# A sliding-window attention and MLP kernel on one core: normalisation split in two, a plain weight cast, shifted V by DMA, a padded first key block

## The chip, the cores and the metric

The kernel runs on one core of a Trainium2 chip. The metric is the device time of the program in microseconds (us); lower is better. A *span* is the time from the first to the last instruction of one profiled execution; it is about 1.7 us shorter than the time of the same run. Most runs of a kernel agree within about 1%; runs over 1.5% above the fastest of their kernel count as slow and are left out of the ratios (the medians are of all runs).

The engines are named as the profile names them: PE is TensorE (matrix products), PEld its weight loads, DVE is VectorE, ACT is ScalarE, POOL is GpSimd, SP is SyncE, which here issues the loads and stores. In the traces of this case each engine takes up its own instructions in program order and waits where an operand is not ready: POOL, for example, once stands idle for 17.15 us in front of one instruction with more work behind it (shown below). The *granted clock* is the share of full speed that the profile records for PE. An *eviction* copies a result of PE out of the memory that PE writes to.

## The reference

Eight batches of 576 rows, 8 heads of 64. Attention looks back over a window of 64 keys, then the rows go through a normalised two-layer MLP with a residual:

```python
scores = q @ k.T / sqrt(64)                    # (8, 8, 576, 576)
mask   = (0 <= i - j) & (i - j < 64)
attn   = softmax(where(mask, scores, -1e9))
x      = (attn @ v) as (8, 576, 512)           # heads side by side

xn  = (x - mean(x)) / sqrt(var(x) + 1e-6) * g_ln      # over the 512
out = x + relu(xn @ w_ch1) @ w_ch2                    # 512 -> 2048 -> 512
```

## The kernel before

Work is cut into 36 blocks of 128 rows. Four blocks form a *group*, and the MLP runs on nine groups of 512 rows. While PE works on the 32 *slots* of group g (16 units of the first layer, then 16 of the second, 4 matmuls each), the attention of batch g+1 is threaded between the slots. The parts that the change and the argument touch (cuts are marked):

```python
def make_vB(b, lo, hi):            # V shifted by 64 rows, for even windows
    nc.vector.tensor_copy(out=vB[b][64:128, lo:hi], in_=vA[b][0:64, lo:hi])
    ...
def w1_cast(i):                    # fp32 -> fp16, times g
    for e in range(2):
        nc.gpsimd.tensor_scalar(out=w1g[...], in0=t[:, e], scalar1=gcol[:, kc:kc+1], op0=ALU.mult)

def s_mm(b, ws):                   # scores of one or two windows, then exp
    k0 = 64 if ws[0] == 0 else 0   # window 0 has no earlier keys: half a key block
    ...
def s_mask(b, ws):                 # DVE: probabilities *= mask
    ...
def b_step(kblk):                  # one block of 128 rows
    # PE: xps = P @ [V, 1], 16 matmuls; then on DVE:
    #   rcp = 1/sum;  xn = xps*rcp;  bn_stats;  bn_aggr -> mean, var
    ...
def group_stats(g):                # DVE, once per group, after its fourth block
    # 12 ops on 128x4: rs = 1/sqrt(var + eps) by two Newton steps
    for kb in range(4):            # z = (xn - mean) * rs
        nc.vector.tensor_scalar(out=z, in0=xn, scalar1=mean, scalar2=rs, ...)
def zt_step(g, pr):                # PE: transposes of two blocks' z; DVE: eviction to zT
    ...
# second layer, per block:         DVE: out = ch + xn, then store

# groups g >= 1, b = g + 1, s0 = 10 (cut):
for i, ws in enumerate([[0], [1, 2], [3, 4], [5, 6], [7, 8]]):
    at(s0 + 2*i, s_mm, b, ws)
    at(s0 + 2*i + 1, s_mask, b, ws)
# b_step of a block 2 slots after the s_mm of its last window
# group_stats 1 slot, zt_step 3 and 4 slots after the group's last block
```

The *fill* is what comes before group 1: loads and casts of W1 and W2, batch 0's attention, then group 0, which also carries batch 1's attention in its second layer.

The softmax here doesn't subtract the row's maximum and nothing guards it: scores larger than these inputs give would overflow.

Of the kernel before, what the change touches and what calls it, by code (L numbers as in the profile page):

```python
# [20 lines left out]
def kernel(  # L21
# [44 lines left out]
    gcol = p_const.tile([128, NKC], FP32, tag="gcol", name="gcol")  # L66
# [6 lines left out]
    x_norm, zT, mvg, zsd = {}, {}, {}, {}  # L73
# [56 lines left out]
    def alloc_vB(b):  # L130
        vB[b] = p_va.tile([128, 5, H, D + 1], FP16, tag="vB", name=f"vB_{b}")

    def make_vB(b, lo, hi):
        nc.vector.tensor_copy(out=vB[b][64:128, lo:hi], in_=vA[b][0:64, lo:hi])
        l1 = max(lo, 1)
        if l1 < hi:
            nc.vector.tensor_copy(out=vB[b][0:64, l1:hi], in_=vA[b][64:128, l1 - 1:hi - 1])
# [13 lines left out]
    def w1_cast(i):  # L151
        q2, pr = divmod(i, 2)
        t = wst.pop(("w1", i))
        for e in range(2):
            kc = 2 * pr + e
            nc.gpsimd.tensor_scalar(  # L156
                out=w1g[:, kc, (HID // 4) * q2:(HID // 4) * (q2 + 1)], in0=t[:, e],
                scalar1=gcol[:, kc:kc + 1], scalar2=None, op0=ALU.mult,
            )
# [11 lines left out]
    def alloc_qkT(b):  # L171
        qkT[b] = [p_qkt.tile([128, NHP, S], FP16, tag=f"qkT{x}", name=f"qkT{x}_{b}") for x in range(2)]
# [7 lines left out]
    def t_main(b, x, half):  # L180
# [5 lines left out]
        evac(x, qkT[b][x][:, 2 * half:2 * half + 2, 0:512].rearrange("c i (p j) -> c i p j", j=4),  # L186
             tp[:, :].rearrange("c i j p -> c i p j"))

    def t_rem(b):
# [6 lines left out]
        for x in range(2):  # L196
            nc.vector.tensor_copy(out=qkT[b][x][:, :, 512:S], in_=tp[:, x])

    def s_mm(b, ws):
        nw = len(ws)  # L200
        k0 = 64 if ws[0] == 0 else 0
        sc = [ps_s.tile([128, NHP, nw, 64], FP32, tag="sc", name=f"sc_{b}_{ws[0]}_{par}") for par in range(2)]
        pt = p_pt.tile([128, 2, NHP, nw, 64], FP16, tag=f"pt{nw}", name=f"pt_{b}_{ws[0]}", bufs=6 if nw == 2 else 3)
        for hp in range(NHP):
            for iw, w in enumerate(ws):
                for par in range(2):
                    rows = slice(64 * par, 64 * par + 64)
                    nc.tensor.matmul(
                        out=sc[par][k0:, hp, iw, :],
                        lhsT=qkT[b][1][rows, hp, max(0, 64 * (w - 1)):64 * (w + 1)],  # L210
# [3 lines left out]
        for par in range(2):  # L214
            nc.scalar.activation(out=pt[k0:, par], in_=sc[par][k0:], func=AF.Exp, bias=0.0, scale=scale)
        for iw, w in enumerate(ws):
            pts[(b, w)] = (pt, iw, k0)

    def s_mask(b, ws):
        pt, _, k0 = pts[(b, ws[0])]  # L220
        m = mask[k0:, :]
        mb = bass.AP(tensor=m.tensor, offset=m.offset, ap=[m.ap[0], [0, 2 * NHP * len(ws)], m.ap[1]])
        ptv = pt[k0:].rearrange("p a h w i -> p (a h w) i")
        nc.vector.tensor_tensor(out=ptv, in0=ptv, in1=mb, op=ALU.mult)

    def v_rhs(b, w, h, k0):
        if w % 2 == 1:
            return vA[b][:, (w - 1) // 2, h, :]
        return vB[b][k0:, w // 2, h, :]

    def b_step(kblk):
# [5 lines left out]
        for h in range(H):  # L237
            par, hp = h % 2, h // 2
            for r, (b, w) in enumerate(halves):
                pt, iw, k0 = pts[(b, w)]  # L240
                nc.tensor.matmul(
                    out=xps[64 * r:64 * r + 64, h, :D + 1],
                    lhsT=pt[k0:, par, hp, iw, :], rhs=v_rhs(b, w, h, k0),
# [11 lines left out]
        nc.vector.bn_aggr(out=mvg[g][:, kb, :], in_=stats)  # L255

    def group_stats(g):
        mv = mvg[g]
        rs = p_grp.tile([128, 4], FP32, tag="rstdg", name=f"rstdg_{g}")
        tmp = p_grp.tile([128, 4, 3], FP32, tag="rstmp", name=f"rstmp_{g}")  # L260
        ve = tmp[:, :, 0]
        hv = tmp[:, :, 1]
        ab = tmp[:, :, 2]
        nc.vector.tensor_scalar(out=ve, in0=mv[:, :, 1], scalar1=EPS, scalar2=None, op0=ALU.add)
        nc.vector.tensor_scalar(out=hv, in0=mv[:, :, 1], scalar1=0.5, scalar2=0.5 * EPS,
                                op0=ALU.mult, op1=ALU.add)
# [5 lines left out]
                                in1=ab.bitcast(I32), op=ALU.subtract)  # L272
        for _ in range(2):
            nc.vector.tensor_tensor(out=ab, in0=rs, in1=rs, op=ALU.mult)
            nc.vector.tensor_tensor(out=ab, in0=ab, in1=hv, op=ALU.mult)
            nc.vector.tensor_scalar(out=ab, in0=ab, scalar1=-1.0, scalar2=1.5, op0=ALU.mult, op1=ALU.add)
            nc.vector.tensor_tensor(out=rs, in0=rs, in1=ab, op=ALU.mult)
        zs = []
        for kb in range(4):
# [63 lines left out]
    for i in range(4):  # L343
        w1_load(i)
# [157 lines left out]
```

## Time and profile before

| | before |
|---|---|
| median time | 420.46 us (4 runs, 417.25 to 421.12) |
| second layer of group 0 starts | 66.2 us |
| first layer of group 1 starts | 99.45 us |
| groups 1 to 6, each | 41.7 to 44.2 us, 258.0 us in sum |
| groups 7 and 8, without attention, and the tail | 28.6, 27.7, about 4 us |

The starts are those of the first-layer matmuls in the timeline of PE. Lines of the page of the kernel before; the second row gives PE's granted clock in tenths, in 40 equal slices of the span:

```profile
span 417.7 us, 6727 instructions
PE 349.5 (84%) x2768; PEld 175.5 (42%) x2768; DVE 203.8 (49%) x440; ACT 139.3 (33%) x243; POOL 101.6 (24%) x107
PEclk9999995898999999899898989999999999999999
```

Busy time in three stretches of the kernel before. The columns are named in the first line, each engine with its instruction count in brackets, then granted clock, share of the DMA engines and GB/s. The first two rows lie in the fill, the third is one steady group:

```profile
core 0: us, PE busy (x) PEld busy (x) DVE busy (x) ACT busy (x) POOL busy (x), PEclk, DMA share, GB/s
20.00:30.00 10.00, 3.94 (x75) 2.81 (x75) 8.52 (x19) 1.74 (x4) 10.00 (x7) 1.00 0.52 161
90.00:100.00 10.00, 4.68 (x44) 2.15 (x42) 8.88 (x27) 0.00 (x0) 0.00 (x0) 0.94 0.10 29
184.96:228.75 43.79, 40.49 (x321) 20.12 (x320) 22.96 (x49) 15.84 (x28) 8.05 (x9) 0.92 0.42 106
```

At 20 to 30 us POOL is busy all the time with W1 and DMA is half idle. At 90 to 100 us DVE is the busy one. In the steady group the clock is only 0.92.

The same group in the chain of waits (start, length, engine, what). `xps` is attention times V, `hps` the first layer, `ch` the second, `pt` the masked probabilities:

```profile
201.44 2.34 PE xps_2342 L241 x16
203.78 1.00 PE hps_15_2369 L308 x4
204.78 1.71 PE ch_0_2376 L321 x4
...
207.03 0.60 PE xps_2403 L241 x16
...
212.24 0.55 DVE z_2449 L282
...
216.53 0.61 DVE pt_7_2464 L224
...
217.18 0.45 PE xps_2542 L241 x15
217.63 4.38 PE ch_1_2526 L321 x12
```

Four second-layer matmuls take 0.86 us elsewhere in this group. The first `xps`, the one with the half key block, takes 2.34 us for 16 matmuls where others take about 0.45 to 0.6; the four `ch_0` matmuls after it take 1.71 us, half speed. Twelve later ones take 4.38 us instead of 2.6. Between them a DVE run (statistics of the group, four z, a mask) holds PE up. A wait of PE in the fill, before the second layer of group 0, for batch 1's last rows of q and k (engine, tile, line, what it waited for: sum, count, longest):

```profile
PE tpr_701 L194 <- POOL qkr_0_1_634 L104: 6.3, 1, 6.3
```

And all of its waits in the steady group above:

```profile
PE xps_2542 L241 <- DVE pt_7_2464 L224: 1.9, 1, 1.9
PE ztp_0_2516 L296 <- DVE z_2449 L282: 1.3, 1, 1.3
```

### The profile page before, as it was taken

The page shows a single profiled execution, that of the slowest core. Times are in us where ns is not written, and L with a number is a line of the kernel's source. Part 1 is how long each engine was busy: PE and PEld are TensorE (multiplying, and loading weights), DVE is VectorE, ACT ScalarE, POOL GpSimd, SP SyncE. Part 2 cuts the span into 40 slices and gives each one's busy share as a digit, 9 for nine tenths or more (in the row PEclk, how much of TensorE's full clock was granted, in tenths as well). Part 3 has the DMA queues.
Part 4 walks back from the last instruction along what each step waited for, and adds up shares of the span by engine and source line. Part 5 has one row for each costly group of instructions (what it writes and reads, how often), then busy time and mean ns, then how long its engine had stood idle before and what let it go on. Part 6 is the DMA issues. An engine that isn't in the chain of part 4 may idle for free.

```text
span 417.7 us, 6727 instructions
## 1 busy us (share of the span) xinstructions
PE 349.5 (84%) x2768; PEld 175.5 (42%) x2768; DVE 203.8 (49%) x440; ACT 139.3 (33%) x243; POOL 101.6 (24%) x107
## 2 busy tenths in 40 slices
PE   1733967976997998699969997899789968999996
PEld 1521432433453544344534543355335433444442
DVE  1488041685559347825492539443944385412001
ACT  2310550222750374016510752057205630440620
POOL 4799946400500250024002320133002000000000
PEclk9999995898999999899898989999999999999999
DMA  8959899604406450458016800872071001102002
GB/s 232 274 166 282 252 268 239 165 27 157 97 2 138 140 163 2 92 127 223 2 42 148 251 2 2 172 234 38 0 171 45 2 2 50 53 0 75 27 25 75
DMA packets 72942, 46.57 MB, mean 111 GB/s; under 512 B 47824, under 2 KB 64208, under 8 KB 72912
## 3 DMA queue, kind: packets, MB, share of 16 engines
q1 hardware_dynamic: 72384, 46.15, 41.3%
q8 instruction: 21, 0.34, 0.4%
q14 instruction: 9, 0.07, 0.1%
q10 hardware_dynamic: 528, 0.00, 0.1%
HBM read 36.70 MB, written 9.44 MB: 110 GB/s over the span
## 4 chain that ended last, share of the span: by engine, by line
PE 60%; DVE 22%; POOL 8%; SPq 4%; DMA 2%; issue 2%; POOLq 0%
POOL w1g L156 6%; SPq L114 3%; PE ch_0_712 L321 1%; DMA w1s_118<-in_moe_w_ch_dram 1%; DMA qk32r_1_273<-in_k_dram 1%; PE ch_1_2526 L321 1%; PE ch_1_2016 L321 1%; POOL w2s L169 1%; PE ch_3_4563 L321 1%; PE ch_2_4543 L321 1%; PE ch_1_4346 L321 1%; PE ch_3_3659 L321 1%; PE ch_2_3121 L321 1%; PE ch_2_2077 L321 1%; PE ch_3_1571 L321 1%
## 5 line engine op out<-in xcount | busy, mean ns | idle before, releaser
L308 PEld LDWEIGHTS <-w1g 128*128 128x128 f16 x576 | 54.0, 99 | 62.6 <-issue 9.0
L321 PEld LDWEIGHTS <-hrT_522 128*128 128x128 f16 x64 | 6.7, 113 | 9.1 <-issue 5.0
L321 PEld LDWEIGHTS <-hrT_2133 128*128 128x128 f16 x64 | 6.6, 107 | 8.5 <-issue 3.0
L321 PEld LDWEIGHTS <-hrT_1599 128*128 128x128 f16 x64 | 6.4, 105 | 8.0 <-issue 2.3
L321 PEld LDWEIGHTS <-hrT_4186 128*128 128x128 f16 x64 | 6.3, 98 | 7.5
L321 PEld LDWEIGHTS <-hrT_4406 128*128 128x128 f16 x64 | 6.2, 97 | 7.6
L327 DVE TENSOR_TENSOR osb_4520<-ch_0_4503,xn_3938 128x512 f32<-128x512 f32 x1 | 0.7, 692 | 16.7 <-PE ch_0_4503 L321 16.7
L321 PEld LDWEIGHTS <-hrT_3687 128*128 128x128 f16 x64 | 6.0, 98 | 6.7
L321 PEld LDWEIGHTS <-hrT_2643 128*128 128x128 f16 x64 | 6.0, 98 | 6.7
L321 PEld LDWEIGHTS <-hrT_3177 128*128 128x128 f16 x64 | 6.0, 98 | 6.7
L321 PEld LDWEIGHTS <-hrT_1089 128*128 128x128 f16 x64 | 5.9, 98 | 6.5
L125 POOL CAST vA_3166<-v_6_3107 128x2048 f16<-128x2048 f32 x1 | 1.9, 1892 | 27.8 <-DMA v_6_3107<-in_v_dram 27.8
L125 POOL CAST vA_2122<-v_4_2063 128x2048 f16<-128x2048 f32 x1 | 1.9, 1892 | 26.2 <-DMA v_4_2063<-in_v_dram 26.2
L125 POOL CAST vA_3676<-v_7_3617 128x2048 f16<-128x2048 f32 x1 | 1.9, 1892 | 25.7 <-DMA v_7_3617<-in_v_dram 25.7
L125 POOL CAST vA_2632<-v_5_2573 128x2048 f16<-128x2048 f32 x1 | 1.9, 1892 | 25.6 <-DMA v_5_2573<-in_v_dram 25.6
L125 POOL CAST vA_1588<-v_3_1529 128x2048 f16<-128x2048 f32 x1 | 1.9, 1893 | 24.0 <-DMA v_3_1529<-in_v_dram 24.0
L178 DVE COPY qkT_1_590<-tp_1_0_607 128x1024 f16<-128x1024 f16 x1 | 1.2, 1224 | 13.2 <-PE tp_1_0_607 L185 13.2
L312 ACT ACTIVATE hrT_2133<-hps_0_2134 128x512 f16<-128x512 f32 x1 | 0.6, 597 | 19.0 <-PE hps_0_2134 L308 19.0
L312 ACT ACTIVATE hrT_2643<-hps_0_2644 128x512 f16<-128x512 f32 x1 | 0.6, 597 | 18.8 <-PE hps_0_2644 L308 18.8
L312 ACT ACTIVATE hrT_522<-hps_0_523 128x512 f16<-128x512 f32 x1 | 0.6, 597 | 17.9 <-PE hps_0_523 L308 17.9
L185 PE MATMUL tp_0_0_143<-ident_99,qk_0_0_0_139 128*128 128x128 f16 x8 | 1.0, 310 | 6.5 <-POOL qk_0_0_0_139 L95 6.5
L296 PE MATMUL ztp_0_502<-ident_99,z_493 128*128 128x128 f16 x4 | 0.6, 308 | 6.7 <-DVE z_493 L282 6.7
(1275 smaller groups left out, 952.6 us busy)
## 6 DMA issues: line engine op xcount, KB each, us to landing
v_0_113<-in_v_dram SPq DMA_DIRECT2D x4, 256.0 KB, 7.5
v_1_262<-in_v_dram SPq DMA_DIRECT2D x4, 256.0 KB, 7.1
v_2_812<-in_v_dram SPq DMA_DIRECT2D x4, 256.0 KB, 5.2
v_3_1529<-in_v_dram SPq DMA_DIRECT2D x4, 256.0 KB, 4.6
v_4_2063<-in_v_dram SPq DMA_DIRECT2D x4, 256.0 KB, 4.3
v_5_2573<-in_v_dram SPq DMA_DIRECT2D x4, 256.0 KB, 4.5
v_6_3107<-in_v_dram SPq DMA_DIRECT2D x4, 256.0 KB, 4.5
v_7_3617<-in_v_dram SPq DMA_DIRECT2D x4, 256.0 KB, 5.6
```

What stands on the lines that cost most here:

```text
L114: nc.sync.dma_start(out=v32[b][:, c], in_=v[b, :, 128 * c:128 * c + 128, :].rearrange("h s d -> s h d"),)
L125: nc.gpsimd.tensor_copy(out=vA[b][:, c0:c1, :, 0:D], in_=v32[b][:, c0:c1])
L156: nc.gpsimd.tensor_scalar(out=w1g[:, kc, (HID // 4) * q2:(HID // 4) * (q2 + 1)], in0=t[:, e], scalar1=gcol[:, kc:kc + 1], scalar2=None, op ...
L169: nc.gpsimd.tensor_copy(out=w2s[:, 2 * i:2 * i + 2, :], in_=wst.pop(("w2", i)))
L178: nc.vector.tensor_copy(out=out, in_=in_)
L185: nc.tensor.transpose(out=tp[:, i, j, :], in_=src[:, i, j], identity=ident16)
L296: nc.tensor.transpose(out=ztp[:, kc, i, :], in_=zs[2 * pr + i][:, 128 * kc:128 * (kc + 1)], identity=ident16)
L308: nc.tensor.matmul(out=hps, lhsT=w1g[:, kc, 128 * hc:128 * (hc + 1)], rhs=zT[g][:, kc, :], start=(kc == 0), stop=(kc == NKC - 1),)
L312: nc.scalar.activation(out=hrT[:, hc, :], in_=hps, func=AF.Relu, bias=0.0, scale=1.0)
L321: nc.tensor.matmul(out=ch[kb], lhsT=hrT[:, hc, 128 * kb:128 * (kb + 1)], rhs=w2s[:, hc, :], start=(hc == 0), stop=(hc == NHC - 1),)
L327: nc.vector.tensor_tensor(out=o, in0=ch[kb], in1=x_norm[kblk][:, :, :].rearrange("p h d -> p (h d)"), op=ALU.add,)
```

## The change

Its intent: take GpSimd's slow W1 multiply out of the fill, dissolve the DVE run at the end of each group, take copies off DVE, and stop PE from alternating between half and whole key blocks. Since 1/sqrt(var + eps) is positive, it commutes with the ReLU and both matrix products, so it can be applied once at the output. The diff, cut to its core:

```diff
-        nc.vector.tensor_copy(out=vB[b][64:128, lo:hi], in_=vA[b][0:64, lo:hi])
+        nc.gpsimd.dma_start(out=vB[b][64:128, lo:hi], in_=vA[b][0:64, lo:hi])
         ...
-        for e in range(2):
-            nc.gpsimd.tensor_scalar(... scalar1=gcol[:, kc:kc + 1], op0=ALU.mult)
+        nc.gpsimd.tensor_copy(out=w1g[:, 2*pr:2*pr+2, ...], in_=t)        # W1 plain
         ...
+        nc.gpsimd.memset(vB[b][0:64, 0], 0.0)                 # in alloc_vB
+        nc.gpsimd.memset(qkT[b][1][:, :, 0:64], 0.0)          # in alloc_qkT: 64 zero keys
-        k0 = 64 if ws[0] == 0 else 0
-        lhsT=qkT[b][1][rows, hp, max(0, 64 * (w - 1)):64 * (w + 1)]
+        lhsT=qkT[b][1][rows, hp, 64 * w:64 * w + 128]
         ...
+        # in b_step, per block:  z = (xn - mean) * g
+        nc.vector.scalar_tensor_tensor(out=z, in0=xn, scalar=mean, in1=gB, ...)
         ...
     def group_stats(g):            # 3 ops on DVE, then 9 on GpSimd; no z
-            nc.vector.tensor_tensor(out=ab, in0=rs, in1=rs, op=ALU.mult)  # and so on
+            nc.gpsimd.tensor_tensor(out=ab, in0=rs, in1=rs, op=ALU.mult)  # and so on
         ...
-                nc.vector.tensor_tensor(out=o, in0=ch[kb], in1=xn, op=ALU.add)
+                nc.vector.scalar_tensor_tensor(out=o, in0=ch[kb], scalar=rstd, in1=xn,
+                                               op0=ALU.mult, op1=ALU.add)
         ...
+        at(13, group_stats, g)
-            t0, s0 = 0, 10
+            t0, s0, sp = 0, 6, 3          # groups >= 1; group 0: 10, 20, 2
-                si = s0 + 2 * ((lastw + 1) // 2) + 2
+                si = s0 + sp * ((lastw + 1) // 2) + 3
                 at(min(si, 32), b_step, kblk)
+                at(max(min(si + 4, 32), ...), zt_step, kblk)
```

More of the change, by code (lines that the diff above doesn't have):

```diff
@@ L65 @@
     magt = p_const.tile([128, 4], FP32, tag="magt", name="magt")
-    gcol = p_const.tile([128, NKC], FP32, tag="gcol", name="gcol")
+    gB = p_const.tile([128, DM], FP32, tag="gB", name="gB")
     w1g = p_const.tile([128, NKC, HID], FP16, tag="w1g", name="w1g")
@@ L72 @@
     qkT, vA, vB, pts = {}, {}, {}, {}
-    x_norm, zT, mvg, zsd = {}, {}, {}, {}
+    x_norm, zT, mvg, zsd, rstd = {}, {}, {}, {}, {}
     def load_qk(b, half):
@@ L131, in alloc_vB @@
         vB[b] = p_va.tile([128, 5, H, D + 1], FP16, tag="vB", name=f"vB_{b}")
+        nc.gpsimd.memset(vB[b][0:64, 0], 0.0)
     def make_vB(b, lo, hi):
-        nc.vector.tensor_copy(out=vB[b][64:128, lo:hi], in_=vA[b][0:64, lo:hi])
-        l1 = max(lo, 1)
-        if l1 < hi:
-            nc.vector.tensor_copy(out=vB[b][0:64, l1:hi], in_=vA[b][64:128, l1 - 1:hi - 1])
+        nc.gpsimd.dma_start(out=vB[b][64:128, lo:hi], in_=vA[b][0:64, lo:hi])
+        l0, l1 = max(lo - 1, 0), min(hi - 1, 4)
+        nc.gpsimd.dma_start(out=vB[b][0:64, l0 + 1:l1 + 1], in_=vA[b][64:128, l0:l1])
     wst = {}
@@ L153, in w1_cast @@
         t = wst.pop(("w1", i))
-        for e in range(2):
-            kc = 2 * pr + e
-            nc.gpsimd.tensor_scalar(
-                out=w1g[:, kc, (HID // 4) * q2:(HID // 4) * (q2 + 1)], in0=t[:, e],
-                scalar1=gcol[:, kc:kc + 1], scalar2=None, op0=ALU.mult,
-            )
+        nc.gpsimd.tensor_copy(
+            out=w1g[:, 2 * pr:2 * pr + 2, (HID // 4) * q2:(HID // 4) * (q2 + 1)], in_=t,
+        )
     def w2_load(i):
@@ L171, in alloc_qkT @@
     def alloc_qkT(b):
-        qkT[b] = [p_qkt.tile([128, NHP, S], FP16, tag=f"qkT{x}", name=f"qkT{x}_{b}") for x in range(2)]
+        qkT[b] = [p_qkt.tile([128, NHP, S + 64 * x], FP16, tag=f"qkT{x}", name=f"qkT{x}_{b}") for x in range(2)]
+        nc.gpsimd.memset(qkT[b][1][:, :, 0:64], 0.0)
     def evac(x, out, in_):
@@ L185, in t_main @@
                 nc.tensor.transpose(out=tp[:, i, j, :], in_=src[:, i, j], identity=ident16)
-        evac(x, qkT[b][x][:, 2 * half:2 * half + 2, 0:512].rearrange("c i (p j) -> c i p j", j=4),
+        evac(x, qkT[b][x][:, 2 * half:2 * half + 2, 64 * x:64 * x + 512].rearrange("c i (p j) -> c i p j", j=4),
              tp[:, :].rearrange("c i j p -> c i p j"))
@@ L196, in t_rem @@
         for x in range(2):
-            nc.vector.tensor_copy(out=qkT[b][x][:, :, 512:S], in_=tp[:, x])
+            nc.vector.tensor_copy(out=qkT[b][x][:, :, 64 * x + 512:64 * x + S], in_=tp[:, x])
     def s_mm(b, ws):
         nw = len(ws)
-        k0 = 64 if ws[0] == 0 else 0
         sc = [ps_s.tile([128, NHP, nw, 64], FP32, tag="sc", name=f"sc_{b}_{ws[0]}_{par}") for par in range(2)]
@@ L208, in s_mm @@
                     nc.tensor.matmul(
-                        out=sc[par][k0:, hp, iw, :],
-                        lhsT=qkT[b][1][rows, hp, max(0, 64 * (w - 1)):64 * (w + 1)],
+                        out=sc[par][:, hp, iw, :],
+                        lhsT=qkT[b][1][rows, hp, 64 * w:64 * w + 128],
                         rhs=qkT[b][0][rows, hp, 64 * w:64 * w + 64],
@@ L214, in s_mm, with v_rhs @@
         for par in range(2):
-            nc.scalar.activation(out=pt[k0:, par], in_=sc[par][k0:], func=AF.Exp, bias=0.0, scale=scale)
+            nc.scalar.activation(out=pt[:, par], in_=sc[par], func=AF.Exp, bias=0.0, scale=scale)
         for iw, w in enumerate(ws):
-            pts[(b, w)] = (pt, iw, k0)
+            pts[(b, w)] = (pt, iw)
     def s_mask(b, ws):
-        pt, _, k0 = pts[(b, ws[0])]
-        m = mask[k0:, :]
+        pt, _ = pts[(b, ws[0])]
+        m = mask[:, :]
         mb = bass.AP(tensor=m.tensor, offset=m.offset, ap=[m.ap[0], [0, 2 * NHP * len(ws)], m.ap[1]])
-        ptv = pt[k0:].rearrange("p a h w i -> p (a h w) i")
+        ptv = pt[:, :].rearrange("p a h w i -> p (a h w) i")
         nc.vector.tensor_tensor(out=ptv, in0=ptv, in1=mb, op=ALU.mult)
-    def v_rhs(b, w, h, k0):
+    def v_rhs(b, w, h):
         if w % 2 == 1:
             return vA[b][:, (w - 1) // 2, h, :]
-        return vB[b][k0:, w // 2, h, :]
+        return vB[b][:, w // 2, h, :]
     def b_step(kblk):
@@ L239, in b_step @@
             for r, (b, w) in enumerate(halves):
-                pt, iw, k0 = pts[(b, w)]
+                pt, iw = pts[(b, w)]
                 nc.tensor.matmul(
                     out=xps[64 * r:64 * r + 64, h, :D + 1],
-                    lhsT=pt[k0:, par, hp, iw, :], rhs=v_rhs(b, w, h, k0),
+                    lhsT=pt[:, par, hp, iw, :], rhs=v_rhs(b, w, h),
                     start=True, stop=True,
@@ L255, in b_step, with zt_step @@
         nc.vector.bn_aggr(out=mvg[g][:, kb, :], in_=stats)
+        z = p_blk.tile([128, DM], FP16, tag="z", name=f"z_{kblk}")
+        zsd[kblk] = z
+        nc.vector.scalar_tensor_tensor(
+            out=z, in0=xn[:, :, :].rearrange("p h d -> p (h d)"), scalar=mvg[g][:, kb, 0:1], in1=gB,
+            op0=ALU.subtract, op1=ALU.mult,
+        )
+    def zt_step(kblk, eng=None):
+        g, kb = divmod(kblk, 4)
+        z = zsd.pop(kblk)
+        if g not in zT:
+            zT[g] = p_grp.tile([128, NKC, 512], FP16, tag="zT", name=f"zT_{g}")
+        ztp = ps_t.tile([128, NKC, 128], FP16, tag="tp", name=f"ztp_{kblk}")
+        for kc in range(NKC):
+            nc.tensor.transpose(out=ztp[:, kc, :], in_=z[:, 128 * kc:128 * (kc + 1)], identity=ident16)
+        dst = zT[g][:, :, 128 * kb:128 * kb + 128]
+        if eng == "act":
+            nc.scalar.copy(out=dst, in_=ztp)
+        else:
+            nc.vector.tensor_copy(out=dst, in_=ztp)
     def group_stats(g):
+        rstd[g] = p_grp.tile([128, 4], FP32, tag="rstdg", name=f"rstdg_{g}")
+        rs = rstd[g]
         mv = mvg[g]
-        rs = p_grp.tile([128, 4], FP32, tag="rstdg", name=f"rstdg_{g}")
-        tmp = p_grp.tile([128, 4, 3], FP32, tag="rstmp", name=f"rstmp_{g}")
-        ve = tmp[:, :, 0]
-        hv = tmp[:, :, 1]
-        ab = tmp[:, :, 2]
+        tmp = p_grp.tile([128, 3, 4], FP32, tag="rstmp", name=f"rstmp_{g}")
+        ve, hv, ab = tmp[:, 0], tmp[:, 1], tmp[:, 2]
         nc.vector.tensor_scalar(out=ve, in0=mv[:, :, 1], scalar1=EPS, scalar2=None, op0=ALU.add)
-        nc.vector.tensor_scalar(out=hv, in0=mv[:, :, 1], scalar1=0.5, scalar2=0.5 * EPS,
-                                op0=ALU.mult, op1=ALU.add)
         nc.vector.tensor_scalar(
@@ L272, in group_stats @@
                                 in1=ab.bitcast(I32), op=ALU.subtract)
+        nc.gpsimd.tensor_scalar(out=hv, in0=mv[:, :, 1], scalar1=0.5, scalar2=0.5 * EPS,
+                                op0=ALU.mult, op1=ALU.add)
         for _ in range(2):
-            nc.vector.tensor_tensor(out=ab, in0=rs, in1=rs, op=ALU.mult)
-            nc.vector.tensor_tensor(out=ab, in0=ab, in1=hv, op=ALU.mult)
-            nc.vector.tensor_scalar(out=ab, in0=ab, scalar1=-1.0, scalar2=1.5, op0=ALU.mult, op1=ALU.add)
-            nc.vector.tensor_tensor(out=rs, in0=rs, in1=ab, op=ALU.mult)
-        zs = []
-        for kb in range(4):
-            kblk = 4 * g + kb
-            z = p_blk.tile([128, DM], FP16, tag="z", name=f"z_{kblk}")
-            nc.vector.tensor_scalar(
-                out=z, in0=x_norm[kblk][:, :, :].rearrange("p h d -> p (h d)"),
-                scalar1=mv[:, kb, 0:1], scalar2=rs[:, kb:kb + 1],
-                op0=ALU.subtract, op1=ALU.mult,
-            )
-            zs.append(z)
-        zsd[g] = zs
-        zT[g] = p_grp.tile([128, NKC, 512], FP16, tag="zT", name=f"zT_{g}")
-    def zt_step(g, pr):
-        zs = zsd[g]
-        ztp = ps_t.tile([128, NKC, 2, 128], FP16, tag="tp", name=f"ztp_{g}_{pr}")
-        for i in range(2):
-            for kc in range(NKC):
-                nc.tensor.transpose(out=ztp[:, kc, i, :], in_=zs[2 * pr + i][:, 128 * kc:128 * (kc + 1)],
-                                    identity=ident16)
-        nc.vector.tensor_copy(out=zT[g][:, :, 256 * pr:256 * pr + 256],
-                              in_=ztp[:, :, :, :].rearrange("p k i t -> p k (i t)"))
+            nc.gpsimd.tensor_tensor(out=ab, in0=rs, in1=rs, op=ALU.mult)
+            nc.gpsimd.tensor_tensor(out=ab, in0=ab, in1=hv, op=ALU.mult)
+            nc.gpsimd.tensor_scalar(out=ab, in0=ab, scalar1=-1.0, scalar2=1.5, op0=ALU.mult, op1=ALU.add)
+            nc.gpsimd.tensor_tensor(out=rs, in0=rs, in1=ab, op=ALU.mult)
     def mlp_units(g):
@@ L326, in l2 @@
                 o = p_blk.tile([128, DM], FP32, tag="osb", name=f"osb_{kblk}")
-                nc.vector.tensor_tensor(
-                    out=o, in0=ch[kb], in1=x_norm[kblk][:, :, :].rearrange("p h d -> p (h d)"), op=ALU.add,
+                nc.vector.scalar_tensor_tensor(
+                    out=o, in0=ch[kb], scalar=rstd[g][:, kb:kb + 1],
+                    in1=x_norm[kblk][:, :, :].rearrange("p h d -> p (h d)"), op0=ALU.mult, op1=ALU.add,
                 )
@@ L342 @@
     load_v(0, 0, 4)
+    nc.sync.dma_start(out=gB, in_=bass.AP(tensor=moe_g_ln.tensor, offset=moe_g_ln.offset, ap=[[0, 128], [1, DM]]))
     for i in range(4):
         w1_load(i)
-    nc.scalar.dma_start(out=gcol, in_=moe_g_ln.rearrange("(kc p) -> p kc", p=128))
     make_identity(nc, ident16)
+    nc.vector.memset(mask, 1.0)
     nc.vector.memset(magt, RSQRT_MAGIC)
-    nc.vector.memset(mask, 1.0)
     alloc_v(0)
@@ L364 @@
             t_main(0, x, half)
+    alloc_vB(0)
     for c in range(4):
         cast_v(0, c, c + 1)
+        if c % 2 == 1:
+            make_vB(0, c - 1, c + 1)
     for i in range(4):
@@ L390 @@
     cast_v(1, 0, 4)
-    alloc_vB(0)
     sets0 = [[0], [1, 2], [3, 4], [5, 6], [7]]
     s_mm(0, sets0[0])
-    for i in range(1, 5):
+    s_mm(0, sets0[1])
+    s_mask(0, sets0[0])
+    for i in range(2, 5):
         s_mm(0, sets0[i])
         s_mask(0, sets0[i - 1])
-        make_vB(0, i - 1, i)
-        if i >= 2:
-            b_step(i - 2)
+        b_step(i - 2)
+        if i >= 3:
+            zt_step(i - 3, "act")
     s_mask(0, sets0[4])
     b_step(3)
-    group_stats(0)
-    zt_step(0, 0)
-    zt_step(0, 1)
+    zt_step(2, "act")
+    zt_step(3, "act")
     for g in range(NGRP):
@@ L421 @@
             at(15, s_mask, 0, [8])
-            t0, s0 = 10, 20
+            t0, s0, sp = 10, 20, 2
         else:
-            t0, s0 = 0, 10
+            t0, s0, sp = 0, 6, 3
         if b < B:
@@ L431 @@
             at(t0 + 5, t_rem, b)
-            at(s0 + 1, alloc_vB, b)
-            at(s0 + 1, make_vB, b, 0, 5)
+            at(s0 - 1, alloc_vB, b)
+            at(s0 - 1, make_vB, b, 0, 5)
             sets = [[0], [1, 2], [3, 4], [5, 6], [7, 8]]
             for i, ws in enumerate(sets):
-                at(s0 + 2 * i, s_mm, b, ws)
-                at(s0 + 2 * i + 1, s_mask, b, ws)
+                at(s0 + sp * i, s_mm, b, ws)
+                at(s0 + sp * i + 1, s_mask, b, ws)
             first, last = (NW * b) // 2, (NW * (b + 1)) // 2
-            for i, kblk in enumerate(range(first, last)):
+            for kblk in range(first, last):
                 lastw = (2 * kblk + 1) - NW * b
-                si = s0 + 2 * ((lastw + 1) // 2) + 2
+                si = s0 + sp * ((lastw + 1) // 2) + 3
                 at(min(si, 32), b_step, kblk)
-                if kblk % 4 == 3:
-                    gg = kblk // 4
-                    if gg == b:
-                        at(min(si + 1, 32), group_stats, gg)
-                        at(min(si + 3, 32), zt_step, gg, 0)
-                        at(min(si + 4, 32), zt_step, gg, 1)
-        elif b == B:
-            at(4, group_stats, b)
-            at(8, zt_step, b, 0)
-            at(9, zt_step, b, 1)
+                at(max(min(si + 4, 32), 17 if kblk // 4 > b else 0), zt_step, kblk)
         if b + 1 < B:
```

## The prediction

> **What bounds it now.** TensorE. The chain of waits gives PE 60%, DVE 22%. By the stretches of busy time: 0 to 99 us is fill (PE 1 to 9 us busy of every 10), 99 to 358 us six nearly equal groups of 42 to 44 us, then two groups without attention at 28 us each.
>
> *Steady group, 185.1 to 228.9 us (43.8 us), from the chain.* At full clock: 128 MLP matmuls at 0.216 us = 27.6; q/k transposes 4x0.45 + 0.34; scores about 2.0; attention-times-V 4.5 blocks x 0.45; z transposes about 1.0: sum about 35. The other 8 us: PE waits for z (1.3) and for a mask multiply (1.9), both behind a DVE run of about 9 us (stats, 13 tiny ops at 0.2, four z, two evictions, output add) that all lands at once; the block with a half key window takes 2.34 us instead of 0.45, its matmuls 0.146 us apart, alternating 64- and 128-row weights; and after such gaps the clock drops: the next 4 matmuls took 1.71 us, 12 later ones 4.38 (0.36 each against 0.216). The Trainium skill names both: "TensorEngine Tiling (Array Packing)", Key Properties (changing the tiling mode drains the array) and "TensorE: Matmul & The Clock Gate", Part 1 (half rate after idle). The trace agrees.
>
> *Fill.* GpSimd's W1 multiplies (16, about 1.6 us each, 25 us) pace W1 and the weight loads behind it until 42 us; DMA is only about half busy at 20 to 30 us. PE then waits 6.3 us (until 65.3) for the last q/k remainder load of batch 1, and the second layer starts cold at 66.3. Group 1 starts at 99.45, after a DVE-bound stretch (8.9 of 10 us).
>
> **What the change does.**
> 1. W1 cast: 8 copies of 128x1024. The like W2 casts take about 1.0, so 8 instead of 25 us. The fill becomes DMA-bound: about 15.5 MB at 28 MB per 100 us ends about 57 us (64.6 before): 8 us won, not 17.
> 2. Padding removes the 64/128 alternation: 1.9 us x 8 batches, and the clock drop behind it.
> 3. z per block, transposes 4 slots later, sets 3 slots apart: the DVE burst is dissolved and zT is ready by slot 25 of 32. Removes 3 to 4 us of PE waits per group and their cold matmuls. z should cost about 0.7 (as the output adds of two tensors, 0.69) instead of 0.46: affordable.
> 4. V copies (1.0+1.7 us per batch on DVE) go to DMA, 0.6 MB per batch. Issued right after the V cast, well before use.
> 5. Rsqrt chain moves mostly to GpSimd, needed only at the output add 6 slots later: off the path.
>
> **Sum.** Second layer of group 0 from about 58; 16 slots plus attention, DVE-limited and partly cold: group 1 at about 84 (was 99.5). Six groups at about 35.8 (was 43): 299. Two at 27.7: 355. Tail 3.8: span 359, time about 360 us (-14%). Range 348 to 375. Faster 0.97, within 2% 0.02, slower 0.01.
>
> **What would show it.** Groups of 35 to 37 us; granted clock near 1.00 after 100 us; first-block attention-times-V near 0.45 us; almost no PE waits on DVE after 100 us; W1 casts ended by about 30 us; PE's wait before the second layer still there, ended by DMA at about 57.
>
> **What could make it wrong.** V copies landing late (group 0 above all, sharing engines with loads of batch 2) stall PE and cool the clock; GpSimd issues them itself, in order behind casts that wait for loads; DVE's slower z contending with GpSimd; scores at 3-slot spacing delaying the ReLU evictions on ACT.

## The result, and the profile after

| | before | predicted | after |
|---|---|---|---|
| median time | 420.46 us | 360 (348 to 375) | 387.37 us (4 runs, 385.84 to 387.73) |
| second layer of group 0 starts | 66.2 | 58 | 62.4 |
| group 1 starts | 99.45 | 84 | 92.0 |
| groups 1 to 6, each | 41.7 to 44.2 | 35.8 | 37.5 to 40.3 |
| their sum | 258.0 | 215 | 232.4 |
| what follows | about 60 | 60 | 59.6 |

The ratio is 0.922 (95% interval 0.917 to 0.927). Ratios are the mean time of one kernel's fast runs over that of the other's of the same rounds, so not quite the ratio of the medians quoted. The change is clearly faster, but the time lies above the range: the profiled span is 384.1 us where 359 were forecast. Of these 25 us, 8 are lost before group 1 and 17 in the six steady groups.

The page of the kernel after:

```profile
span 384.1 us, 6774 instructions
PE 323.3 (84%) x2768; PEld 162.6 (42%) x2768; DVE 189.6 (49%) x350; ACT 140.4 (37%) x247; POOL 121.9 (32%) x216
PEclk9999996996999999999999999999999999999999
```

The same three stretches. The third is again one steady group, but group 4, with five blocks of attention, where the one before was group 3, with four; group 4 of the kernel before lasted 44.2 us, with DVE busy for 25.0:

```profile
20.00:30.00 10.00, 4.61 (x81) 3.33 (x81) 7.37 (x15) 2.82 (x6) 5.61 (x6) 1.00 1.03 327
90.00:100.00 10.00, 8.36 (x56) 4.98 (x57) 4.09 (x7) 4.21 (x6) 0.00 (x0) 0.70 0.87 248
209.64:248.65 39.01, 35.38 (x342) 18.13 (x341) 24.89 (x46) 15.74 (x28) 12.43 (x22) 1.00 0.56 134
```

DMA is now full at 20 to 30 us, the clock is 1.00 in the group, and PE needs 35.4 us of busy time for it, as the prediction had summed up. But the group lasts 39.0 us. DVE is busy for 24.9 us of it, which looks like room enough. The chain of waits shows why it is not:

```profile
221.34 0.42 PE xps_2820 L238 x16
...
223.70 0.75 DVE z_2843 L255
224.45 0.61 DVE pt_1_2800 L221
225.11 0.47 PE xps_2886 L238 x16
...
228.74 0.61 DVE pt_3_2866 L221
229.40 0.47 PE xps_2980 L238 x16
...
231.81 1.07 DVE z_3004 L255
232.88 1.45 DVE pt_5_2960 L221
234.37 0.47 PE xps_3052 L238 x16
...
239.17 0.45 PE xps_3102 L238 x16
```

This is a loop. A block's matmuls (`xps`, first now 0.42 us) release its DVE chain: reciprocal, x, statistics, z, about 2.6 us. The mask of the *next* set (`pt`) stands behind that chain in DVE's queue, although its scores have long been ready, and the next block's matmuls wait for that mask. This order is not new: the kernel before has the next mask one slot behind a block too (block 2 slots after its scores, sets 2 slots apart). The change kept it, and put z into the chain. One turn takes 3.8 to 5.0 us here (starts 221.34, 225.11, 229.40, 234.37, 239.17), while PE has only about 3.7 us of other work for three slots (estimate: 3 x 0.86 for the MLP, 0.43 for scores, 0.45 for the block, 0.22 for transposes, durations of the same trace). Who waited in this group, all of PE's waits:

```profile
PE xps_3102 L238 <- DVE pt_7_3032 L221: 1.4, 1, 1.4
PE xps_3052 L238 <- DVE pt_5_2960 L221: 1.3, 1, 1.3
PE xps_2980 L238 <- DVE pt_3_2866 L221: 0.6, 1, 0.6
PE xps_2886 L238 <- DVE pt_1_2800 L221: 0.4, 1, 0.4
```

Their sum, 3.7 us, is the whole surplus of the group. Over the six groups PE waits 18.7 us, all of it for masks (20 waits): the waits for z are gone, those for masks are not (17.2 us before). The turn that ends at 234.37 is longer because z and the mask are slow there: 1.07 us instead of 0.75, and 1.52 instead of 0.68 in the timeline. The one that ends at 239.17 has a slow z again (1.08) and an output add of 0.74 us in front of its mask. In these turns POOL casts q and k of the next batch, and casts that meet a slow operation are slowed too. Group 6, which has nothing left to cast, has no z over 0.75 and no mask over 0.69 us; it lasts 37.5 us, and PE still waits 2.0 us for masks. So the order alone costs about 2 us a group, the slowed operations the rest. POOL's timeline in this group (in brackets how long it was idle before, and what ended that):

```profile
228.83 0.57 POOL L290 TENSOR_TENSOR rstmp_2922<-rstdg_2921 128x4 f32<-128x4 f32 x1 [17.15 <-DVE rstdg_2921 L285]
...
231.29 1.04 POOL L95 CAST qk_0_6_0_3156<-qk_0_6_0_2911 128x1024 f16<-128x1024 f32 x1
232.28 1.50 POOL L95 CAST qk_1_6_0_3158<-qk_1_6_0_2913 128x1024 f16<-128x1024 f32 x1
233.72 1.50 POOL L95 CAST qk_0_6_1_3174<-qk_0_6_1_2948 128x1024 f16<-128x1024 f32 x1
```

and DVE's:

```profile
231.81 1.07 DVE L255 SCALAR_TENSOR_TENSOR z_3004<-xn_2979,mvg_3002,gB 128x512 f16<-128x512 f32 x1
232.80 1.52 DVE L221 TENSOR_TENSOR pt_5_2960<-pt_5_2960,mask 128x1024 f16<-128x1024 f16 x1
```

The reciprocal root that moved to GpSimd waits 17.15 us for three small DVE operations at slot 13, and the casts stand behind it in POOL's queue. In the kernel before, casts of a group ran in its first 14 us (190.7 to 198.6 in the group that began at 185), ahead of the DVE run. The Trainium skill, "SBUF — State Buffer", section "SBUF: two separate sides", says that VectorE and GpSimd share one pair of SBUF ports, that an instruction holds it to its end, and that a VectorE operation with two SBUF inputs contends with a GpSimd operation that reads SBUF. Both slow operations have two SBUF inputs, and the times fit: the mask, 0.68 us alone, ends half a microsecond (0.54) after the cast that began before it.

In the fill, PE's waits between 60 us and the start of group 1, the two longest:

```profile
PE tpr_697 L192 <- POOL qkr_0_1_616 L104: 5.7, 1, 5.7
PE ztp_1079 L267 <- DVE z_1070 L255: 3.2, 1, 3.2
```

The first is the wait for batch 1's last rows, still there; the second is for block 8's z, which only group 2 needs, just ahead of group 1's first layer.

### The profile page after: what moved, and what is told of

Read it like the earlier page. It is cut to its first block, busy times and chain, and to the rows that moved or that the text cites. A ratio compares the mean times of both kernels' runs of the same rounds, so it can differ in the third digit from the quotient of the medians.

```text
span 384.1 us, 6774 instructions
## 1 busy us (share of the span) xinstructions
PE 323.3 (84%) x2768; PEld 162.6 (42%) x2768; DVE 189.6 (49%) x350; ACT 140.4 (37%) x247; POOL 121.9 (32%) x216
## 4 chain that ended last, share of the span: by engine, by line
PE 55%; DVE 26%; DMA 8%; SPq 6%; issue 3%; POOL 1%; ACT 0%; POOLq 0%
SPq L114 3%; DMA w1s_125<-in_moe_w_ch_dram 3%; DMA w2s_234<-in_moe_w_ch_dram 2%; DMA qk_0_1_1_214<-in_q_dram 2%; DMA qk32r_1_272<-in_k_dram 1%; PE ch_0_708 L315 1%; SPq L79 1%; PE ch_3_4604 L315 1%; PE ch_2_2087 L315 1%; PE ch_1_4564 L315 1%; PE ch_3_4413 L315 1%; PE ch_1_4373 L315 1%; PE ch_2_4196 L315 1%; PE ch_2_3667 L315 1%; PE ch_3_3185 L315 1%
## 5 line engine op out<-in xcount | busy, mean ns | idle before, releaser
L315 PEld LDWEIGHTS <-hrT_4433 128*128 128x128 f16 x64 | 6.3, 98 | 7.6
L315 PEld LDWEIGHTS <-hrT_4242 128*128 128x128 f16 x64 | 6.2, 98 | 7.6
L321 DVE SCALAR_TENSOR_TENSOR osb_4370<-ch_0_4353,rstdg_4327,xn_3495 128x512 f32<-128x512 f32 x1 | 0.8, 751 | 16.2 <-PE ch_0_4353 L315 16.2
L321 DVE SCALAR_TENSOR_TENSOR osb_4561<-ch_0_4544,rstdg_4518,xn_3949 128x512 f32<-128x512 f32 x1 | 0.8, 750 | 16.2 <-PE ch_0_4544 L315 16.2
L315 PEld LDWEIGHTS <-hrT_503 128*128 128x128 f16 x64 | 5.8, 103 | 6.8 <-issue 1.9
L290 POOL TENSOR_TENSOR rstmp_1316<-rstdg_1315 128x4 f32<-128x4 f32 x2 | 0.8, 386 | 24.5 <-DVE rstdg_1315 L285 24.4
L290 POOL TENSOR_TENSOR rstmp_4519<-rstdg_4518 128x4 f32<-128x4 f32 x2 | 0.4, 198 | 25.4 <-DVE rstdg_4518 L285 25.3
L315 PEld LDWEIGHTS <-hrT_3729 128*128 128x128 f16 x64 | 5.8, 98 | 6.0
L315 PEld LDWEIGHTS <-hrT_2665 128*128 128x128 f16 x64 | 5.8, 98 | 6.0
L315 PEld LDWEIGHTS <-hrT_1085 128*128 128x128 f16 x64 | 5.8, 98 | 6.0
L315 PEld LDWEIGHTS <-hrT_3213 128*128 128x128 f16 x64 | 5.8, 98 | 6.0
L315 PEld LDWEIGHTS <-hrT_1601 128*128 128x128 f16 x64 | 5.8, 98 | 6.0
L315 PEld LDWEIGHTS <-hrT_2149 128*128 128x128 f16 x64 | 5.8, 97 | 6.0
L306 ACT ACTIVATE hrT_3729<-hps_0_3730 128x512 f16<-128x512 f32 x1 | 0.6, 597 | 15.5 <-PE hps_0_3730 L302 15.5
L306 ACT ACTIVATE hrT_3213<-hps_0_3214 128x512 f16<-128x512 f32 x1 | 0.6, 597 | 15.5 <-PE hps_0_3214 L302 15.5
L306 ACT ACTIVATE hrT_2665<-hps_0_2666 128x512 f16<-128x512 f32 x1 | 0.6, 597 | 15.5 <-PE hps_0_2666 L302 15.5
L306 ACT ACTIVATE hrT_1601<-hps_0_1602 128x512 f16<-128x512 f32 x1 | 0.6, 597 | 15.5 <-PE hps_0_1602 L302 15.5
L306 ACT ACTIVATE hrT_2149<-hps_0_2150 128x512 f16<-128x512 f32 x1 | 0.6, 597 | 15.5 <-PE hps_0_2150 L302 15.5
L290 POOL TENSOR_TENSOR rstmp_2922<-rstdg_2921 128x4 f32<-128x4 f32 x2 | 0.8, 386 | 17.2 <-DVE rstdg_2921 L285 17.2
L290 POOL TENSOR_TENSOR rstmp_1858<-rstdg_1857 128x4 f32<-128x4 f32 x2 | 0.8, 386 | 17.2 <-DVE rstdg_1857 L285 17.1
```

What stands on the lines that cost most here:

```text
L290: nc.gpsimd.tensor_tensor(out=ab, in0=rs, in1=rs, op=ALU.mult)
L306: nc.scalar.activation(out=hrT[:, hc, :], in_=hps, func=AF.Relu, bias=0.0, scale=1.0)
L315: nc.tensor.matmul(out=ch[kb], lhsT=hrT[:, hc, 128 * kb:128 * (kb + 1)], rhs=w2s[:, hc, :], start=(hc == 0), stop=(hc == NHC - 1),)
L321: nc.vector.scalar_tensor_tensor(out=o, in0=ch[kb], scalar=rstd[g][:, kb:kb + 1], in1=x_norm[kblk][:, :, :].rearrange("p h d -> p (h d)"), ...
```

## The experiments

Theory A: the place of the mask in DVE's queue, behind the block's chain, sets the pace. Rival B: DVE simply has too much work in that stretch, in whatever order. Theory C: the root on GpSimd harms by holding up the casts. All but e7, e8, e9 start from the changed kernel. "Group 1" is the start of group 1's first layer, "six groups" the length of groups 1 to 6, both from the profiled run.

| run | group 1 | six groups | median us | ratio to before |
|---|---|---|---|---|
| the change | 92.0 | 232.4 | 387.37 | 0.922 |
| e12, the change again | 97.6 | 231.8 | 387.42 | 0.923 |
| e1 blocks one slot later | 97.4 | 215.5 | 370.94 | 0.882 |
| e2 casts before the root | 92.0 | 225.4 | 381.72 | 0.904 |
| e3 zT evictions on ACT | 90.8 | 233.3 | 385.27 | 0.915 |
| e4 V copies on DVE | 89.3 | 233.3 | 385.40 | 0.916 |
| e5 = e1 + e2 | 90.7 | 214.6 | 371.55 | 0.887 |
| e14 = e5 + block 8 later | 90.6 | 214.2 | 367.53 | 0.876 |
| e6 = e14 + fill reordered | 87.6 | 214.3 | 362.50 | 0.863 |
| e11 block 8 later | 90.7 | 233.0 | 385.31 | 0.917 |
| e8 before + plain W1 cast | 91.0 | 255.3 | 411.67 | 0.980 |
| e7 before + padding, zeroing late | 129.1 | 243.7 | 435.28 | 1.038 |

The two profiles of the changed kernel show how to read it: the steady groups repeat within 0.6 us in sum, the fill differs by 5.5 us between two executions. So the steady groups are compared by their lengths, the fill only by ratios of times. The groups of the kernel before repeat less well: e8, which leaves them alone, has 255.3 us where the kernel before has 258.0, with a granted clock of 1.00 in groups 2 and 3 against 0.96 and 0.92. So the lengths of e7's groups are good to about 3 us. e9, e10 and e13 are not in the table, as their profiled runs counted as slow.

### e1: the block one slot later

```diff
-                si = s0 + sp * ((lastw + 1) // 2) + 3
+                si = s0 + sp * ((lastw + 1) // 2) + (4 if g else 3)
```

In the same slot a mask is issued ahead of a block, so the next mask now stands before the block's chain. The transposes of a block's z move with it. No work is added or removed.

> Edit: in groups 1 to 6 each attention-times-V block is issued one slot later, so that the mask multiply of the next set stands ahead of the block's chain (reciprocal, x, stats, z) in VectorE's queue, not behind it. Theory A (order: mask -> block -> 3 us chain -> next mask is a loop through VectorE's in-order queue, and sets the pace at about 4.4 us a block): the PE waits on masks (about 4 us per group) mostly go, groups fall from 37.5 to 40.2 us to about 36, time 387 -> about 372 us. Rival B (VectorE simply has too much work in that stretch): the waits move to other tiles, groups change by under 0.7 us, time within 4 us of 387.

Measured: 370.94 us, groups of 35.1 to 36.8. One steady group of e1, busy time, and all waits of PE in it:

```profile
205.75:242.22 36.47, 35.85 (x342) 17.57 (x341) 24.29 (x46) 15.52 (x28) 13.02 (x23) 1.00 0.60 143
```

```profile
PE ztp L267 <- DVE z L255: 0.3, 1, 0.3
PE xps L238 <- DVE xn L247: 0.3, 1, 0.3
```

DVE's busy time is nearly the same (24.3 us against 24.9), PE's waits on masks are gone: over the six groups it waits 1.2 us in all, against 18.7. In this group one z still takes 1.59 us and one mask 1.10, next to casts, and PE does not wait for it. Theory A is shown and rival B falls: the whole surplus of the six groups, 232.4 - 215.5 = 17 us, goes away with one slot of order.

### e2: the casts before the root

The loads of q and k of the next batch go to slot 6 and their casts to slots 8 to 10 in groups 1 to 5, ahead of the root at slot 13.

```diff
-            at(12, load_qk, n, 0)
+            at(12 if g == 0 else 6, load_qk, n, 0)
             ...
-            at(24, cast_qk, n, 0)
+            at(24 if g == 0 else 8, cast_qk, n, 0)
             ...
```

> Edit: in groups 1 to 5 the q/k loads and casts of the next batch are issued before the reciprocal-root chain, so GpSimd does not hold them behind it. Theory C (the chain moved to GpSimd blocks its in-order queue for 17 us and pushes the casts into the VectorE-bound stretch, where z takes 1.07 instead of 0.75 us and one mask 1.5 instead of 0.68): z and mask return to 0.75 and 0.68, the groups 1 to 5 lose about 1.5 us each, time -6 to -8 us. If those casts only cost VectorE time that PE does not wait for: under 2 us.

Measured: 381.72 us, the six groups 7.0 us shorter (232.4 to 225.4), as theory C had it. Five groups have casts, so 1.4 us each. z and masks are back at 0.75 and 0.68 us nearly everywhere (some early ones are slow now, one mask of group 4 with 1.53), and PE's waits in the six groups fall from 18.7 to 12.1 us. No wait of PE there ends at the root itself; what the root did to the queue behind it was on the path.

### e3: evictions of zT on ACT

```diff
-    def zt_step(kblk, eng=None):
+    def zt_step(kblk, eng="act"):
```

> Edit: all evictions of z's transposes on ScalarE instead of VectorE (0.42 us each, 4 to 5 per group). Theory A: these evictions are not in the loop (they run while PE does the next block), so within 3 us of 387. Rival B (amount of VectorE work): about 1.7 us less VectorE work per group, so -6 us or more.

The six groups take 233.3 us, no shorter, with some 1.7 us less DVE work in each. This again speaks for A against B: work off the loop is worth nothing. The time is 2 us lower; since the groups are not, that is in the fill, where this run's size is within what two profiles of one kernel differ by. No more is claimed for it.

### e4: V copies back on DVE

```diff
-        nc.gpsimd.dma_start(out=vB[b][64:128, lo:hi], in_=vA[b][0:64, lo:hi])
+        nc.vector.tensor_copy(out=vB[b][64:128, lo:hi], in_=vA[b][0:64, lo:hi])
         # and the other half alike
```

> Edit: the shifted V copies go back from DMA to VectorE, as they were before the change. If the on-chip DMA is worth what it took off VectorE (about 2.7 us per batch) on the path: +8 us or more. If, as the trace suggests, VectorE idles at that slot (5) of groups 1 to 6: within 3 us of 387 or a little faster, since the first block then need not wait 3.6 us for a DMA in the fill (which ends at a DMA anyhow); group 0 may get up to 3 us longer.

The six groups take 233.3 us, so the on-chip DMA is worth nothing in the steady groups: at slot 5 DVE is idle anyway. In the fill, where PE waited 3.6 us for that DMA, the copies on DVE did no harm: the ratio is 0.916 against 0.923.

### e5: both

> Edit: the edits of e1_block_later and e2_casts_before_rsqrt together, on the changed kernel. If order (A) and the held-up casts (C) are two causes of one surplus, the sum is capped by TensorE's own work (about 35 us per group): groups 35.0 to 35.8, time 368 to 371 us, that is at most 3 us below e1 alone. If they were independent: 371 - 6 = 365.

Groups of 34.9 to 37.1 us, 214.6 in sum, 1 us below e1: the two are causes of one surplus, not independent. Once the mask no longer waits behind the chain, DVE has slack and the slowed operations cost little.

### e7 and e9: the padding alone, on the kernel before

```diff
+        nc.gpsimd.memset(qkT[b][1][:, :, 0:64], 0.0)
+        nc.gpsimd.memset(vB[b][0:64, 0], 0.0)
-        k0 = 64 if ws[0] == 0 else 0
+        k0 = 0
         # and the padded key offsets
```

> Edit: the kernel before, with the padded first key block alone (64 zero key columns, 64 zero V rows). Theory of the prediction (1.9 us per batch of drained array, and the half-rate clock that follows): first-block attention-times-V at 0.45 instead of 2.34 us, 420 -> 400 to 405 us. If VectorE's run sets the pace there anyhow (as in the changed kernel): the 1.9 us turn into waits for VectorE, time above 414 us.

Measured 435.28 us, slower than before. The edit was at fault: in the kernel before `alloc_vB(0)` comes late, so the zeroing stood behind all casts of the fill. The longest wait of PE:

```profile
PE xps L243 <- POOL vB L132: 47.8, 1, 47.8
```

The steady groups still tell what was asked: 243.7 us in sum against 258.0, 14.3 us less, give or take the 3 us named above. PE's waits in them are much as before (27.2 us against 28.2), so the gain is in the matmuls themselves. With that one call moved forward:

> Edit: as e7_padding_alone, with the zeroing of batch 0's V rows put before the first casts in GpSimd's queue (in e7 it stood behind 54 us of casts, and PE waited 47.8 us for it). In e7 the six groups took 40 to 41 us each against 41.7 to 44.2 before: 14.3 us less in sum. If that holds and the fill is that of before: 420 -> about 405 us. If the fill loses what the groups won: above 414.

Measured: 404.69 us, ratio 0.960 (95% interval 0.953 to 0.968), 14 to 20 us won. The prediction had 15.2 us for the drained array (8 times 1.9) and gave no figure for the clock, so the size of this part was right. Padding alone does not keep the clock up: it is 0.96 in groups 3 and 4 of e7.

### e8: the plain W1 cast alone, on the kernel before

```diff
-        for e in range(2):
-            nc.gpsimd.tensor_scalar(... scalar1=gcol[:, kc:kc + 1] ...)
+        nc.gpsimd.tensor_copy(out=w1g[:, 2*pr:2*pr+2, ...], in_=t)
```

The result is wrong, as g is missing.

> Edit: the kernel before, with W1 cast plainly and g left out (the result is wrong on purpose). The prediction's 8 us: second layer of group 0 at 58 instead of 66.3 us, time 412. If, as in the changed kernel, the fill's loads then end at about 60 us: second layer at about 62, time 415 to 418 us.

Measured: 411.67 us, ratio 0.980 (0.974 to 0.986), so 6 to 11 us won; against a threshold of 2% this counts as unclear. In the profiled run, the fastest of the four, the second layer starts at 60.75, 5.5 us earlier than before, and group 1 at 91.0, about as early as with the whole change (92.0 and 97.6). So nothing shows that the rest of the change won time in the fill.

### e11 and e12: block 8 later, and the change again

Block 8 belongs to group 2. It moves from slots 31 and 32 of group 0 to slots 1 and 5 of group 1:

```diff
+            if g == 1:
+                at(1, b_step, 8)
+                at(5, zt_step, 8)
             for kblk in range(first, last):
+                if kblk == 8:
+                    continue
```

> Edit: the changed kernel, with block 8 alone moved from the end of group 0 (slots 31, 32) into group 1 (slots 1 and 5). The trace of the changed kernel has PE wait 3.2 us for that block's z before group 1's first layer. If it is on the path: group 1 starts 3 us earlier, time 387 -> 384. If the VectorE run of group 1 gives it back: 387.

> The changed kernel as it is, in the same rounds, to compare the others with: 387 us, within 2.

Measured: 385.31 against 387.42 us in the same rounds, 2.1 us, with intervals that overlap. From second layer to group 1 this profile has 25.9 us, against 29.7 and 30.7 in the two profiles of the change. The expected 3 us are not more than indicated.

### e6, e10 and e14: a version that beats both

e6 is e5 with block 8 later (and the other blocks of group 0 one slot later), and with the fill reordered: V and remainders of batch 1 are loaded before the second half of W2, their shifted copies issued at once, scores of batch 1 from slot 15, its last transpose at slot 24.

```diff
     cast_v_rem(0)
+    make_vB(0, 4, 5)
+    load_v(1, 0, 4); load_v_rem(1); load_qk_rem(1)
     for i in range(4):
         w2_cast(i)
         w2_load(i + 4)
-    load_v(1, 0, 4)
+    cast_v(1, 0, 4); cast_v_rem(1); make_vB(1, 0, 5)
     ...
-            t0, s0, sp = 10, 20, 2
+            t0, s0, sp = 10, 15, 3
-            at(t0 + 5, t_rem, b)
+            at(t0 + 5 if g else 24, t_rem, b)
```

> Edit: e5_both, and in the fill: V and the remainders of batch 1 are loaded before the second half of W2, their shifted copies are issued right after the cast, batch 1's scores start at slot 15 instead of 20 with 3-slot spacing, the remainder transpose waits until slot 24, and block 8 (needed by group 2 only) moves from the end of group 0 into group 1. Theory D (the 29.8 us from second layer to group 1 are a wait for the batch 1 remainders, then a VectorE-bound run of five blocks, and both can be started earlier): second layer starts at about 56 us instead of 62.4, group 1 at about 80 instead of 92, time about 358 us. If the fill is DMA-bound to its end whatever the order: group 1 not before 88, time over 366.

Measured: 362.50 us, ratio 0.863, correct. Group 1 came at 87.6, not at 80. The timeline of PE shows a new wait, of the padding's own making:

```profile
64.06 0.39 PE L205 MATMUL sc<-qkT,qkT 64*128 64x64 f16 x8 [9.02 <-POOL qkT L170]
```

The zeroing of batch 1's key columns stood behind the W2 casts in POOL's queue. e10 issues it early:

```diff
     alloc_v(1)
     alloc_vB(1)
+    alloc_qkT(1)
```

> Edit: as e6_fill_reordered, with the zeroing of batch 1's key columns issued early too (in e6 the scores of batch 1 waited 9.0 us, until 64.1, for that memset behind the W2 casts). Theory D: the second layer then starts at 56 to 58 us, waits a little for the last part of W2 (landed at 62.7 in e6), group 1 at 81 to 83, time 356 to 358 us. If the last W2 loads bind: group 1 at 86 or later, time above 360.

Measured: 363.96 us, ratio 0.864, the same as e6. So removing this wait did not help, as the second alternative had it. The profiled run of e10 counted as slow, so its lengths are not read here; but in kind its waits fit: none for that zeroing is left, and PE waits for casts of W2 instead (4.5 us in two waits).

> Edit: e5_both, with block 8 moved into group 1 as in e11. If the two add: 371 - 2 = 369 us. If the loads' order of e6 and e10 is worth the rest of their gain, these stay 5 us or more ahead; if block 8 is, this one reaches 363 to 365 too.

e14, without the reordered loads, took 367.53 us, ratio 0.876. By the ratios block 8 adds to e5 (0.887 to 0.876), and the reordered fill adds again (0.863). The intervals of e5 and e14 overlap a little (0.882 to 0.892, 0.869 to 0.883) and their two profiles start group 1 at the same time, so the first step is indicated, not shown; those of e14 and e6 (0.858 to 0.869) just meet.

### e13: half of W2 not loaded

```diff
-    ... in_=wst.pop(("w2", i)))
+    ... in_=wst[("w2", i % 4)])       # the second half reads the first half's tiles
-        w2_load(i + 4)
```

The result is wrong.

> Edit: the changed kernel, but the second half of W2 (2 MB of the fill's about 15.5) is not loaded; its casts read the tiles of the first half again (the result is wrong on purpose). If the fill is bound by the rate of the DMA (28 MB per 100 us): the last remainder of batch 1 and the second layer come about 7 us earlier (55 to 60 instead of 62 to 67), time about 380. If waits in the queues bind: under 2 us.

Measured on its two fast runs: 380.72 and 377.57 us, ratio 0.902 (0.893 to 0.912) against 0.923 for the change. Taking away 2 MB, by estimate 7 us at 28 MB per 100 us, brought about 9 us (0.021 x 420). The two runs left out as slow, 383.56 and 384.14 us, had no lower clock (0.989 and 0.988 against 0.985 and 0.991); with them it is nearer 6. Both fit a fill that is bound by its loads, and so does the share of the DMA engines over the first 60 us, 1.01 and 0.95 in the two profiles of the changed kernel. The edit also takes four loads out of SP's queue, ahead of batch 1's; bytes and queue are not told apart here.

## Why the prediction was wrong, point by point

- **The bound of the steady group at full clock, about 35 us: right.** PE's busy time in one is 35.4 us after the change, and e1 brings groups of 35.1 to 36.8.
- **Padding (point 2): right.** The first block takes 0.42 us instead of 2.34, and alone the padding is worth 4% (e9). The clock in the group is 1.00 instead of 0.92 with the whole change, but not with padding alone (0.96 in two groups of e7). Of the two pages cited in the prediction, the one on tiling held; what the trace adds to the one on the clock is in the last section.
- **The DVE run dissolved (point 3): this step failed.** It said that spacing of 3 slots "removes 3 to 4 us of PE waits per group". It removed 1.6 us: 28.2 us of waits in six groups became 18.7. The waits for z went (11.0 us with the one for zT), but the prediction put the wait for a mask down to the same DVE run, and that was wrong: the masks' waits stayed (17.2 and 18.7 us). Their cause is the order inside DVE's queue, which was not followed: a mask falls one slot behind a block, before the change and after it, so every mask waits for a block's chain, and the next block for that mask: 3.7 us of waits in the group shown, 17 us of length in six groups. e1 takes them away without changing any work.
- **z at about 0.7 us: right** (0.75). The Trainium skill, "VectorE: DVE Perf Modes", section "The perf-mode tier table", has fp32 `tensor_tensor` at the base rate and fp32 `tensor_scalar` at up to twice that. It has no row for z's new instruction, scalar and tensor in one, but the trace fits the same step: 0.55 us for z with two scalars in the timeline of before, 0.75 with a second tensor. What the prediction called affordable lies on the loop.
- **The root on GpSimd "off the path" (point 5): wrong.** No wait of PE in the steady groups ends at the root, but it held POOL's queue for 17 us and pushed casts into the DVE-bound stretch. Worth 7 us while the loop is there (e2), about 1 us without it (e5). The prediction named contention with GpSimd as a risk, but not what would cause it.
- **V copies (point 4): harmless, but worth nothing** in the steady groups (e4).
- **W1 cast (point 1): right in kind, mis-sized in the change.** Alone it is worth 6 to 11 us (e8), where 8 were predicted. But in the changed kernel the last load of batch 1's rows landed at about 60.3 us (issued at 55.2, 5.1 us to landing), not at the estimated 57, against 64.6 before: 4 us won, not 8. The second layer began at 62.4 us (66.9 in e12), not 58. The mechanism, a fill bound by loads, is what e13 supports.
- **From second layer to group 1, 26 us: mis-sized** by 4; it measured 29.7. e11 has 25.9 with block 8 out of the way, which the sum had left out as five blocks' chains on DVE, not four. The time gained by that was only 2 us, so this is indicated, not shown.

Open stays why the fill's loads take a different time from run to run (DMA moved 276 and 259 GB/s over the first 60 us in two profiles of the changed kernel), and what binds group 1's start in e6 and e10 after the reordering (the waits of e10 point to the casts of W2).

## What to carry to other kernels

An engine that is busy 64% of a stage can still set its pace, if its queue holds an instruction that others wait for behind one that waits for others: follow the order in the queue around one turn of the loop before calling work affordable. An operation moved to a less busy engine brings its waits along, and everything behind it in that queue waits too; even a memset can (47.8 us in e7). Test order first: it costs one number in the schedule, and here it was worth 4%.

## What the Trainium skill lacked or had wrong

- "TensorEngine Tiling (Array Packing)", Key Properties, says that a change of tiling mode drains the array, but not what that costs. In the kernel before, 16 matmuls alternating 64- and 128-row weights took 2.34 us, 0.146 us each, against 0.42 us for 16 of one mode after.
- "TensorE: Matmul & The Clock Gate", Part 1, explains half rate by idle windows of about 3.4 us, and further down by short idle times between groups of matmuls; drains are not named. In the kernel before, half-rate matmuls (1.71 us for four) came 1 us after the drained block, with no wait of PE ahead of them in that group, so a stretch with a drained block can be followed by half rate without a wait. It is not always so: of the six drained blocks in groups 1 to 6, this one and that of group 4 were followed by 3.41 us of half rate without a wait, the others were not.
- "SBUF — State Buffer", "SBUF: two separate sides", says that the loser of the shared ports is blocked for the other's instruction. In the fill of the changed kernel a mask of 128x512, about 0.42 us alone, took 2.65 us while three casts of 1.04 us followed each other: the loser was not served between them. Seen in one other profile too, e11.
- "VectorE: DVE Perf Modes", "The perf-mode tier table", has no row for the instruction of one scalar and two tensors (scalar_tensor_tensor): 128x512 fp32 to fp16 took 0.75 us here, against 0.55 us for the form with two scalars.
- No page that we used tells how far the rate of the same loads varies between executions: 276 and 259 GB/s here.
